# Second sequence's first layer: one product by inner products over pairs of units, and three steps moved to the layer in front

## The chip, the cores and the metric

The kernel runs on one core of one Trainium2 chip. The metric is the device time of that core in microseconds (us), lower is better; the time before is the median of three runs.

## What is computed

Four sequences of 768 rows go through routing attention and then through a feed-forward block. The attention part (8 heads of width 64; a query sees only the keys that fall to the same of 16 centroids) yields `x` with shape (4, 768, 512). The part that the change is about comes after it:

```python
mu = np.mean(x, axis=-1, keepdims=True)
var = np.mean((x - mu) ** 2, axis=-1, keepdims=True)
xn = (x - mu) / np.sqrt(var + 1e-06) * g_ln
ch = np.maximum(xn @ w_ch1, 0.0) @ w_ch2      # 512 -> 2048 -> 512
return (x + ch).astype(np.float32)
```

Everything is float32. The first layer is the product with `w_ch1`, the second the product with `w_ch2`.

## The kernel before

After the attention of all four sequences (b = 0 to 3), the kernel computes the feed-forward block sequence by sequence, first layer, then second layer. Hidden values are kept transposed: 128 hidden channels on the partitions, rows of the sequence in the free dimension.

Both layers use a fast 2 by 2 scheme (seven products of half-size blocks in place of eight). In the first layer of every sequence the halves are: inputs 0 to 255 and 256 to 511, hidden channels 0 to 1023 and 1024 to 2047, rows of the sequence in two halves of 384. A unit j (0 to 7) is 128 hidden channels of each half. Its seven products are the parts 1 to 7 of `first_layer` (L898): each is two float32 matmuls of 128x384 into one PSUM bank (`product`, L851). Part 1 and part 2 together give the hidden tile (0, j): part 1 (`x_ps`) is copied out by ScalarE (ACT) as `p1`, part 2 (`y_ps`) is added to it by VectorE (DVE) in `add_relu` (L885). Part 5 (`z_ps`) and the sums s1 to s4 of blocks of `w1` (`w1_sums`, L647, four DVE instructions of 128x256) and t1 to t4 of blocks of `xn` (`x_sum`) serve the others.

The last two sequences (`paired_layer`, b = 2 and 3) go one level deeper in some of the seven products: two neighbouring units, the two input blocks of 128 and the two halves of the 384 rows form a 2 by 2 scheme again, so that four matmuls of 128x384 become seven of 128x192 (`inner_products`, L1279, its matmul L1287). The operands of that are built by DVE: `inner_x` (L1249, four instructions of 128x192) from the rows, `w_sums` (L1257, four of 128x128) from the weights; each product's result is added onto another or put in its place by DVE (128x192 from PSUM).

The second layer is plain 2 by 2 for b = 0 (`second_layer`, L995) and two levels deep for b = 1 to 3 (`deep_layer`, L1532; 49 products of four matmuls of 128x192). The deep layer reads its weights from DRAM through a ring of ten tiles. What lies there is prepared once: `w2_sum` makes four sums of `w2`, `w2_keep` stores them, `w2_back` reads them again, and `w2_split` (L1065) turns each of seven blocks into four differences (four DVE instructions of 128x512) and stores them to `w2_d` (one DMA of 1 MB on SP).

Order of the work: inside `tc.manual_schedule` the engines named there execute in the order of the source. In the second layer of b = 0 these are TensorE (PE) and DVE; jobs for the gaps stand in the table `jobs` by (part, tt). In the first layer of b = 1 (`first_units`, L1664, and `unit_end`, L1781) they are PE, DVE, ACT and SP. For each unit j the order of parts is 1, 2, then part 4 of unit j - 1, 6, part 3 of unit j - 1, 5, 7. Between them stand: the norm statistics of the next sequence (ACT, L573 to L575), `w1_sums` of the next unit, `outer_sums` of the unit before (L1105), a transpose of columns every second unit (L518), and, at the end of each unit but the last, one `w2_split`, in the order of blocks 1, 5, 3, 4, 2, 7, 6. The check that the shortcut's assumptions hold (`all_in_range`, L806: fourteen short DVE instructions) comes after unit 0, its flag after unit 2.

Room in SBUF: tile `wt` of `w2_split` has two buffers. Pool `splits` is opened where pool `early` of the layer in front is closed, and takes over its room.

Of the kernel before, what the change touches and what calls it, by code (L numbers as in the profile page):

```python
# [23 lines left out]
def kernel(  # L24
# [873 lines left out]
    def first_layer(b, j, part):  # L898
# [26 lines left out]
        elif part == 3:  # L925
            alone = "z" not in st
            if alone:
                st["z"] = ps("y_ps")
            product(st["z"], s4, x_block(b, 1, 1), alone)
            add_relu(1, j, st["z"], st["u2"])  # L930

# [133 lines left out]
    def w2_split(m, src):  # L1065
# [3 lines left out]
        t = splits.tile([P, 4, NQH, P], F32, tag="wt", name="wt", bufs=2)  # L1069
        t1, t2, t3, t4 = [t[:, i] for i in range(4)]  # L1070
        for o, x, y in ((t1, b12, b11), (t2, b22, t1), (t3, b22, b12), (t4, b21, t2)):
            nc.vector.tensor_tensor(o, x, y, ALU.subtract)
        return lambda: nc.sync.dma_start(
            out=w2_d[ORDER.index(m)].rearrange("w p f -> p w f"), in_=t.rearrange("p w c f -> p w (c f)")
        )
# [245 lines left out]

    def deep_room(b):
# [69 lines left out]
    def paired_layer(b):  # L1392
# [67 lines left out]
        def onto_first(j, l):  # L1460
            h = place((1, l))[:, j : j + 2].rearrange("p c t -> p (c t)")
            nc.vector.tensor_tensor(h, fifth_sum, h, ALU.add)
            if l:
                summed.extend(hidden_tile(1, NFH + j + r) for r in range(2))
# [5 lines left out]
        for g in range(NPU):  # L1470
            j = 2 * g
            plan = inner_plan(g, last)
            for slot, (r, part) in enumerate(OUTER[last], 1):
                if (g, slot) != (0, 1):
                    first_layer(b, j + r, part)
                if last and (slot == 7 or slot == 5 and g):
                    onto_first(j, slot // 7)
                for what in plan.get(slot, ()):
# [11 lines left out]
                if not last:  # L1490
                    if g == 0:
# [4 lines left out]
                        if slot == 4:  # L1496
                            x_of[2] = inner_x(x_block(b, 1, 0), pairs_x)
                        if slot == 5:
                            x_sum(b, 4)
                        if slot in (6, 8):  # L1500
                            onto_first(j, slot // 8)
                    elif slot in (5, 7):
                        onto_first(j, slot // 7)
                    if slot == (6 if g else 8):
# [5 lines left out]
                relu(len(summed))  # L1510
# [12 lines left out]
                if g == NPU - 1 and slot in ((6, 8) if last else (9, 10)):  # L1523
                    c = 2 * (slot in (8, 10))
                    inner_sums(deep[b], ORDER[0], cs=slice(c, c + 2))

# [5 lines left out]
    def deep_layer(b, more, st):  # L1532
# [110 lines left out]
        for m, way in STEPS:  # L1643
# [5 lines left out]
            if way == 1:  # L1649
# [12 lines left out]
    deep = {}  # L1662

    def first_units(b, j):  # L1664

        chunks = within.pop(j, []) if b == 0 else []
        for part, ahead in ((1, 0), (2, 0), (4, 1), (6, 0), (3, 1), (5, 0), (7, 0)):
            if chunks and part in (1, 3):
                split_weight(chunks[0])
            if j >= ahead:  # L1670
                first_layer(b, j - ahead, part)
            if part in (4, 6, 3):
                relu(1)
            if b and part == 1 and 0 < j < NT:
                norm_rows(b + 1, j)
            if b and part == 6 and j % 2 and turning:
# [6 lines left out]
            if part == 5:  # L1683
                if j + 1 < NFH:
                    w1_sums(b, j + 1)
                    if b == 0:
                        outer_keep(b, j + 1)
                if b and j:
                    outer_sums(j - 1, j > 4)
# [386 lines left out]
```

## Time and profile before

| what | us |
|---|---|
| median of three runs (876.49 to 877.44) | 876.69 |
| the profiled execution's own time | 876.86 |
| its span in the profile | 874.7 |
| attention, up to the first layer of b = 0 | 0 to 318.7 |
| second layer of b = 0 | 390.0 to 465.1 |
| first layer of b = 1 | 465.1 to 534.9 |
| first layer of b = 2 | 602.5 to 671.4 |

The span is the time from the first to the last recorded instruction. 876.86 less 874.7 is 2.16 us that lie around it. Durations and starts are from this one execution. "Busy" of PE comes from modelled ends of matmuls, so the distance from the start of one group to the start of the next (called pitch below) is the better measure of what a matmul costs. A float32 matmul stands in the trace as two records.

### The profile page before, as it was taken

How to read it: one execution, taken by the hardware profiler on the slowest of the kernel's cores; microseconds unless marked ns; L12 is line 12 of the kernel's file. 1: busy time of each engine (PE TensorE's matmuls, PEld its weight loads, DVE VectorE, ACT ScalarE, POOL GpSimd, SP SyncE). 2: the span in 40 equal slices, each digit the busy share in tenths (PEclk: the TensorE clock that was granted, in tenths of full speed). 3: DMA queues.
4: the chain of work that ended last, by engine and by line, in shares of the span. 5: the costliest groups of instructions: out<-in, count | busy, mean ns of one | idle time of the engine just before them, and what ended most of it. 6: DMA issues, size and time to landing. Idle time of an engine off the chain costs nothing.

```text
span 874.7 us, 13677 instructions
## 1 busy us (share of the span) xinstructions
PE 864.7 (99%) x4768; PEld 590.1 (67%) x4768; DVE 726.0 (83%) x1221; ACT 410.8 (47%) x774; POOL 141.4 (16%) x228
## 2 busy tenths in 40 slices
PE   8999999999999999999999999999999999999996
PEld 5444444444444445568886557998767998778996
DVE  6899999999999878878676878887877897767875
ACT  6777788888888833331003542112563111353110
POOL 1011221222222123220000210002340002350000
PEclk9999999999999999999999999999999999999999
DMA  8777789999986429887685887874567874464865
GB/s 159 140 131 130 135 178 173 206 210 196 208 168 189 122 98 271 257 238 269 163 228 152 269 295 258 283 200 156 156 196 226 295 205 162 134 173 140 274 198 118
DMA packets 229756, 169.65 MB, mean 194 GB/s; under 512 B 159328, under 2 KB 180336, under 8 KB 228656
## 3 DMA queue, kind: packets, MB, share of 16 engines
q1 hardware_dynamic: 194800, 140.50, 58.3%
q0 software_dynamic: 11632, 23.95, 12.4%
q10 hardware_dynamic: 23248, 4.25, 2.7%
q8 instruction: 40, 0.66, 0.3%
q14 instruction: 36, 0.29, 0.1%
HBM read 119.67 MB, written 40.59 MB: 183 GB/s over the span
## 4 chain that ended last, share of the span: by engine, by line
PE 98%; SPq 1%; DMA 1%; issue 0%; ACT 0%; DVE 0%; DVEq 0%
PE x_ps L853 19%; PE s_ps L401 17%; PE a_ps L413 14%; PE x_ps L1161 12%; PE z_ps L1161 6%; PE x_ps L968 5%; PE z_ps L853 5%; PE y_ps L853 4%; PE y_ps L1161 3%; PE x_ps L1287 3%; PE z_ps L968 2%; PE z_ps L1287 1%; PE den_ps L469 1%; PE sim_ps L320 1%; PE y_ps L968 1%; PE y_ps L1287 1%
## 5 line engine op out<-in xcount | busy, mean ns | idle before, releaser
L401 PE MATMUL s_ps<-t,t 64*128 64x384 f32 x768 | 154.8, 483 | 0.0
L401 PEld LDWEIGHTS s_ps<-t,t 64*128 64x128 f32 x768 | 68.0, 187 | 39.0 <-issue 38.3
L1236 POOL DMA_DIRECT2D out_dram<-y x64 | 49.5, 782 | 213.0 <-DVE y L1222 166.7
L1161 PE MATMUL x_ps<-lower,w 128*128 128x192 f32 x448 | 80.5, 326 | 0.0
L1161 PEld LDWEIGHTS x_ps<-lower,w 128*128 128x128 f32 x448 | 74.2, 190 | 0.8
L396 ACT ACTIVATE e<-s_ps 128x768 f32<-128x768 f32 x84 | 67.0, 811 | 7.0 <-PE s_ps L401 6.4
L396 ACT ACTIVATE w<-s_ps 128x768 f32<-128x768 f32 x80 | 64.4, 811 | 8.3 <-PE s_ps L401 7.7
L401 PE MATMUL s_ps<-mask,mask 64*128 64x384 bf16 x384 | 62.8, 323 | 1.0 <-ACT e L396 0.6
L882 ACT COPY p<-x_ps 128x384 f32<-128x384 f32 x32 | 15.3, 477 | 95.3 <-PE x_ps L853 90.0
L413 PE MATMUL a_ps<-e,v_sb 128*64 128x384 f32 x336 | 57.6, 488 | 0.0
L895 ACT ACTIVATE lower<-lower 128x384 f32<-128x384 f32 x88 | 43.7, 518 | 29.1 <-DVE lower L887 19.2
L413 PE MATMUL a_ps<-w,v_sb 128*64 128x384 f32 x320 | 55.2, 488 | 0.0
L853 PE MATMUL x_ps<-xn,w 128*128 128x384 f32 x128 | 46.6, 487 | 0.0
L853 PE MATMUL x_ps<-xn,ws 128*128 128x384 f32 x128 | 46.6, 487 | 0.0
L853 PE MATMUL x_ps<-xt,ws 128*128 128x384 f32 x128 | 46.5, 487 | 0.1
L853 PE MATMUL x_ps<-xt,w 128*128 128x384 f32 x128 | 46.0, 486 | 0.0
L413 PEld LDWEIGHTS a_ps<-e,v_sb 128*64 128x64 f32 x336 | 23.5, 137 | 31.8 <-issue 28.7
L289 POOL DMA_DIRECT2D w<-tb x32 | 28.4, 886 | 90.0 <-DVE tb L286 68.2
L413 PEld LDWEIGHTS a_ps<-w,v_sb 128*64 128x64 f32 x320 | 22.4, 137 | 30.4 <-issue 28.2
L401 PEld LDWEIGHTS <-mask 64*128 64x128 bf16 x384 | 18.9, 94 | 35.0 <-issue 10.0
L1174 ACT COPY u<-x_ps 128x192 f32<-128x192 f32 x30 | 9.6, 318 | 66.4 <-PE x_ps L1161 61.8
L366 ACT ACTIVATE mask<-oh,far 32x384 bf16<-32x384 bf16 x61 | 37.3, 612 | 3.3 <-DVE oh L349 1.9
(314 smaller groups left out, 1840.4 us busy)
## 6 DMA issues: line engine op xcount, KB each, us to landing
w<-w_d SPq DMA_DIRECT2D x84, 256.0 KB, 3.2
raw<-in_moe_w_ch_dram SPq DMA_DIRECT2D x32, 512.0 KB, 5.5
w<-w_t SPq DMA_DIRECT2D x36, 256.0 KB, 5.1
w<-tb POOLq DMA_DIRECT2D x32, 256.0 KB, 5.6
w_d<-wt SPq DMA_DIRECT2D x7, 1024.0 KB, 5.3
w<-w_all SPq DMA_DIRECT2D x27, 256.0 KB, 3.1
v_sb<-in_v_dram SPq DMA_DIRECT2D x32, 192.0 KB, 3.8
xr<-x_d SPq DMA_DIRECT2D x24, 256.0 KB, 3.9
```

Source lines behind the costliest of these rows:

```text
L289: nc.gpsimd.dma_start(out=w, in_=fb, accum_op=ALU.add)
L366: nc.scalar.activation(out, oh[src, :], AF.Identity, bias=add, scale=factor)
L396: nc.scalar.activation(e, s[:, :, :HC], AF.Exp, scale=SCALE)
L401: nc.tensor.matmul(s[:, j, :HC], of_keys[:, keys], of_queries[:, o : o + HC], start=part == first, stop=part != first, skip_group_check=True,)
L413: nc.tensor.matmul(acc[j * D : (j + 1) * D, :HC], loaded[n]["v"][:, j, c, :], e[:, j, :], start=(c == 0), stop=(c == NT - 1),)
L853: nc.tensor.matmul(bank[:, :HC], lhs[:, c, :], rhs[:, c], start=first and c == 0, stop=c == NDH - 1, skip_group_check=True,)
L882: nc.scalar.copy(t, bank[:, :HC])
L895: nc.scalar.activation(h, h, AF.Relu)
L968: nc.tensor.matmul(bank[:, :MH].rearrange("p (h f) -> p h f", h=2), hidden[lhs + (c,)][:, tt * P : (tt + 1) * P], rhs[:, :, c], start=firs ...
L1161: nc.tensor.matmul(bank, w[:, c, :], a[:, c], start=(way in (1, 2, 5) or alone) and c == 0, stop=c == NQH - 1, skip_group_check=True,)
L1236: queues[i % len(queues)].dma_start(out=to, in_=y)
L1287: nc.tensor.matmul(bank, p["w"][way], p["x"][way], start=way in (1, 2, 5), stop=True, skip_group_check=True)
```

## The change

- In the first layer of b = 1, part 2 is no longer made. In its place every pair of units (0 and 1, 2 and 3, and so on) makes the product of the same blocks by seven inner products with `inner_products`, onto the `p1` of both units. `pair_begin` (new) builds their operands: `inner_x` once, `w_sums` once per pair. The order of parts becomes 1, 5, part 4 of unit j - 1, 6, part 3 of unit j - 1, 7, with inner products 1 and 2 after part 6 and 6 and 5 after part 7 of an even unit, 7 after part 5 and 4 and 3 after part 6 of the odd one. `w1_sums` of the next unit comes after part 3 in place of after part 5.
- `w2_split` of blocks 1 and 3 is made in the second layer of b = 0 (`w2_split_ahead`), into two tiles with tag `ws` of two buffers. The others (5, 2, 4, 7, 6) stay, at units 1, 2, 3, 5 and 6; those of units 2 and 6 make two of their four differences one unit later. Each stores 1 MB as two DMAs of 512 KB. Tile `wt` has one buffer in place of two.
- The range check moves to the second layer of b = 0, after product 7 of its second tile.
- `paired_layer`: some steps of b = 2 stand in other slots, and relus are issued one slot later.
- `deep_layer` of b = 1 makes the sums for its first block in its own first steps.

The diff, cut to its core:

```diff
@@ first_layer, part 3, after add_relu(1, j, ...)
+            if alone:
+                summed.pop()
@@
-    def w2_split(m, src):
+    def w2_split(m, src, tiles=None):
...
-        t = splits.tile([P, 4, NQH, P], F32, tag="wt", name="wt", bufs=2)
-        t1, t2, t3, t4 = [t[:, i] for i in range(4)]
-        for o, x, y in ((t1, b12, b11), (t2, b22, t1), (t3, b22, b12), (t4, b21, t2)):
-            nc.vector.tensor_tensor(o, x, y, ALU.subtract)
-        return lambda: nc.sync.dma_start(
-            out=w2_d[ORDER.index(m)].rearrange("w p f -> p w f"), in_=t.rearrange("p w c f -> p w (c f)")
-        )
+        if tiles is None:
+            t = splits.tile([P, 4, NQH, P], F32, tag="wt", name="wt", bufs=1)
+            tiles = [t[:, :2], t[:, 2:]]
+        t1, t2, t3, t4 = [t[:, i] for t in tiles for i in range(2)]
+
+        def make(sums):
+            for o, x, y in sums:
+                nc.vector.tensor_tensor(o, x, y, ALU.subtract)
+
+        make(((t1, b12, b11), (t2, b22, t1)))
+
+        def store():
+            make(((t3, b22, b12), (t4, b21, t2)))
+            for i, t in enumerate(tiles):
+                nc.sync.dma_start(
+                    out=w2_d[ORDER.index(m)][2 * i : 2 * i + 2].rearrange("w p f -> p w f"),
+                    in_=t.rearrange("p w c f -> p w (c f)"),
+                )
+
+        return store
+
+    def w2_split_ahead(m):
+
+        w2_split(m, w2_plain(m), [
+            xpool.tile([P, 4, NDH, P], F32, tag="ws", name="ws", bufs=2).rearrange(
...
+            for _ in range(2)
+        ])()
@@
+    def pair_begin(b, j):
+
+        if j == 0:
+            t = splits.tile([P, 3 * QC], F32, name="pi")
+            pairs_of["parts"] = [t[:, i * QC : (i + 1) * QC] for i in range(3)]
+            pairs_of["x"] = inner_x(x_block(b, 1, 0), splits.tile([P, S], F32, name="xi"))
+            pairs_of["w"] = splits.tile([P, 4 * P], F32, name="wi")
+        (a11, a12), (a21, a22) = blocks = w1_pair(j)
+        w_sums(blocks, parts_of(pairs_of["w"], 4))
+        pairs_of[b, j] = second_pair(
+            b, j, w_operands(a11, a12, a22, pairs_of["w"]), pairs_of["x"], pairs_of["parts"]
+        )
@@ paired_layer, b = 2
+                            inner_keep(3, 0)
...
-                        if slot in (6, 8):
-                            onto_first(j, slot // 8)
+                        if slot in (8, 9):
+                            onto_first(j, slot - 8)
...
-                    if slot == (6 if g else 8):
+                    if slot == 6 and g:
                         inner_keep(3, g)
...
-                relu(len(summed))
+                relu(summed_first)
@@ deep_layer
-            if way == 1:
+            if way == 1 and b < PAIRED and m == ORDER[0]:
+                for cs in (slice(0, NQH - 1), slice(NQH - 1, NQH)):
+                    if cs.start:
+                        inner_sums(st, m, cs=cs)
+                    inner_late(st, m, way, cs)
+            elif way == 1:
@@ first_units
-        for part, ahead in ((1, 0), (2, 0), (4, 1), (6, 0), (3, 1), (5, 0), (7, 0)):
+        parts, sums_after, inner_at = ((1, 0), (2, 0), (4, 1), (6, 0), (3, 1), (5, 0), (7, 0)), 5, {}
+        if b:
+            parts, sums_after = ((1, 0), (5, 0), (4, 1), (6, 0), (3, 1), (7, 0)), 3
+            inner_at = {5: (7,), 6: (4, 3)} if j % 2 else {6: (1, 2), 7: (6, 5)}
+        for part, ahead in parts:
...
+            if part in inner_at:
+                inner_products(pairs_of[b, j - j % 2], inner_at[part])
+                if 3 in inner_at[part]:
+                    summed.extend(hidden_tile(0, j - i) for i in (1, 0))
+                relu(len(summed))
+            if b and part == 1 and j % 2 == 0:
+                pair_begin(b, j)
...
+            if b and part == 6 and halves:
+                halves.pop()()
...
+            if part == (sums_after if j or b == 0 else 6) and j + 1 < NFH:
+                w1_sums(b, j + 1)
...
+            if b and j and part == (3 if j % 2 else 7):
+                outer_sums(j - 1, j > 2)
@@ jobs of the second layer of b = 0
-            (2, 2): [do(norm_rows, 1, 0), do(norm_rows, 1, 1), do(hidden_sums, 4, range(2))],
+            (2, 2): [
+                do(norm_rows, 1, 0), do(norm_rows, 1, 1), do(hidden_sums, 4, range(2)), do(w2_split_ahead, 1),
+            ],
-            (6, 1): [turn_columns],
+            (6, 1): [turn_columns, do(w2_split_ahead, 3)],
-            (7, 1): [do(norm_apply, 1, 0, 2), do(norm_apply, 1, 0, 3)],
+            (7, 1): [do(norm_apply, 1, 0, 2), do(norm_apply, 1, 0, 3), range_check],
@@ unit_end
-                if j == 0:
-                    outer["ends"] = all_in_range()
...
-                m = (1, 5, 3, 4, 2, 7, 6, None)[j]
+                m = (None, 5, 2, 4, None, 7, 6, None)[j]
...
-                if j in (5, 6):
-                    outer_late("s", "e", (0, 0), j - 5)
+                if j == 4:
+                    outer_late("s", "e", (0, 0), 0)
...
-            if b == 1 and m:
-                split()
+            if b == 1:
+                if j % 2 == 0 and m:
+                    halves.append(split)
+                elif m:
+                    split()
```

## Prediction

> **What bounds the kernel now.** I read the page's busy times and the chain, then the stretches around the change, PE's waits, the starts of single matmul groups, and DVE's groups. All lines are of the one profiled execution.
>
> ```profile
> span 874.7 us, 13677 instructions
> PE 864.7 (99%) x4768; PEld 590.1 (67%) x4768; DVE 726.0 (83%) x1221; ACT 410.8 (47%) x774; POOL 141.4 (16%) x228
> ...
> PE 98%; SPq 1%; DMA 1%; issue 0%; ACT 0%; DVE 0%; DVEq 0%
> ```
>
> PE holds the whole chain. Are there gaps in the three stages that the change edits? In the stretches, the columns are length, then busy us of PE, weight load, DVE, ACT:
>
> ```profile
> 390.00:467.50 77.50, 77.50 (x354) 66.73 (x353) 54.13 (x102) 4.33 (x8) 0.00 (x0) 1.00 0.71 203
> 467.50:535.10 67.60, 67.60 (x212) 39.70 (x212) 54.47 (x118) 34.03 (x83) 8.60 (x12) 1.00 0.78 256
> 603.50:671.40 67.90, 67.90 (x269) 47.40 (x268) 53.39 (x133) 38.13 (x103) 18.57 (x24) 1.00 0.58 171
> ```
>
> PE equals the length in each, and the list of PE's waits holds no entry there. Since ends are modelled, I check with starts (start, length, number of records):
>
> ```profile
> 465.05 1.45 PE L853 MATMUL x_ps<-xn,w 128*128 128x384 f32 x4
> 466.34 1.45 PE L853 MATMUL y_ps<-xn,w 128*128 128x384 f32 x4
> 467.63 1.45 PE L853 MATMUL x_ps<-xt,ws 128*128 128x384 f32 x4
> ...
> 619.38 1.45 PE L853 MATMUL x_ps<-xn,w 128*128 128x384 f32 x4
> 620.66 0.49 PE L1287 MATMUL x_ps<-qs 128*128 128x192 f32 x2
> 620.99 0.49 PE L1287 MATMUL z_ps<-qs 128*128 128x192 f32 x2
> 621.32 1.45 PE L853 MATMUL x_ps<-xn,w 128*128 128x384 f32 x4
> ```
>
> A part (two matmuls of 128x384) starts 1.290 after the one before; units of b = 1 follow each other at 9.03 = 7 x 1.290. An inner product takes 0.325 between its neighbours, half of 0.645: a 192-wide matmul pays no extra, also where it stands between wide ones. So this layer is PE work without a gap: time changes by the PE work removed, plus every wait that the change creates.
>
> **What the skill says.** "Perfetto Trace Analysis", Identifying the Most-Contended Engine, warns that matmul busy time is no measure of headroom; hence the starts above. "TensorE: Matmul & The Clock Gate", Step-by-step: what each phase is for, says that the next weights load while a matmul runs; the trace agrees, with 190 ns loads hidden behind 0.162 us records. "VectorE: DVE Perf Modes", TRN2 errata, prices a float32 tensor_tensor at (N + 151)/0.96 ns; the rows below agree (N = 192: 357). "DMA: Bandwidth & Descriptors", Anatomy of one DMA, says that the wait of a DMA is held on the issuing sequencer, so a waiting one holds all behind it on SP; the waits of SP here read that way (L1073 waits 29.7 us in six, for DVE).
>
> **PE, part by part.** Removed: 8 units x 2 matmuls x 0.645 = 10.32. Added: 4 pairs x 7 x 0.325 = 9.10. Net -1.22 us. No other PE work changes; the flag's transpose stays. The operand shapes and the mixture with wide matmuls are those of b = 2, so I see no further price; an unhidden event wait on PE's queue (51 ns, eight in this layer now) is covered there as well.
>
> **DVE in this layer.** Durations:
>
> ```profile
> L1072 DVE TENSOR_TENSOR wt<-w,wt 128x512 f32<-128x512 f32 x6 | 4.1, 688 | 0.1
> L887 DVE TENSOR_TENSOR lower<-y_ps,p 128x384 f32<-128x384 f32 x8 | 4.4, 547 | 2.2 <-PE y_ps L853 2.2
> ...
> L1296 DVE TENSOR_TENSOR pi<-x_ps,p 128x192 f32<-128x192 f32 x12 | 4.3, 356 | 3.9 <-PE x_ps L1287 3.9
> L1265 DVE TENSOR_TENSOR wi<-w 128x128 f32<-128x128 f32 x8 | 2.3, 283 | 0.0
> L1254 DVE TENSOR_TENSOR xi<-xn 128x192 f32<-128x192 f32 x2 | 0.7, 352 | 0.0
> ```
>
> Added: 28 results x 0.356 = 10.0; w_sums 16 x 0.285 = 4.6; inner_x 4 x 0.352 = 1.4; together 16.0. Removed: part 2's adds 8 x 0.547 = 4.4; two splits 8 x 0.687 = 5.5; range check 472.69 to 475.45, 2.8; together 12.7. Net +3.3 on 54.7 of 69.9 (465.05 to 534.94): 58 of 68.7, 84%. Enough room on average, so what counts is order. I laid DVE's order in the new program beside PE's starts at the pitches above:
>
> - Start. `inner_x` writes into room of the closed pool, so it waits until the last `o_sb` store has landed. Before, only the first split (475.67) waited for that. The store is issued at 465.71 and such stores land after 1.8: 467.5. Queued behind on DVE: the sums wi, two results, `w1_sums`(1). Inner 1 and 2 need no sums; s1 of unit 1 is done at 471.0 and wanted at 472.8. Cost 0; the cover is 1.8.
> - PE wants s1 of the next unit after parts 7 and 1, 2.6 after part 3 (5.2 before). The tight place is unit 3: results 4 and 3 (to 496.2), half a split (497.5), transpose (498.4), part 3's add (498.9), s1 at 499.3; PE wants it at 499.5, with its weight load a little earlier. I take 0.1, bounds 0 and 0.4.
> - One `wt` buffer: a split's first instruction now waits for the landing of the store before it. Block 2's stores go out at 497.6; block 4's split is due at 502.3; the 1 MB store's landing in the trace is 5.3:
>
> ```profile
> w_d<-wt SPq DMA_DIRECT2D x7, 1024.0 KB, 5.3
> ```
>
> So 0.6 late, of which 0.4 is cover before PE's inner product 6 of unit 4, which reuses the bank whose result is queued behind. Cost 0.2, bounds 0 and (landing 6.5) 1.4. The distances elsewhere are 6.2 to 6.5 (block 5 to 2, 7 to 6), and over 10 (4 to 7): none late at 5.3.
> - ACT: its copies free the banks; relus that wait for DVE stand behind u2 in odd units and in front of u3. u3 of unit 3 is copied by 500.1, its bank wanted at 500.8. Cost 0.
>
> **What moves to the layer in front.** DVE there is busy 54.1 of 77.5. Two splits (5.5) and the check (2.8) make 62.4. Block 1's split delays the statistics by about 1.5: ready near 425.3, their transpose due at 427.1. In the new SP order the statistics' rows no longer stand behind the store of a `w2` sum (issued 437.03, rows at 437.72, DVE then idle for 4.07 until 443.47); they are issued near 430, so that wait goes and pays for the check. Second tile's product 7 is added before the check; the third's is added by about 447.8, and PE writes its bank again at 451.4. If the rows were as late as before, it would be 450.9: still in time. Block 3's split waits for block 1's stores (made 418.7, wanted 432), and the `ws` room is wanted again only at 463. The two stores pass two row loads and two stores on SP; POOL gets nothing. Cost 0, bounds 0 and 0.5. Deep layer: its first late sum ends near 538.7, wanted at 539.4. Cost 0.
>
> **b = 2.** Its one inner product off the pitch lasts 384 ns against 326: at most 0.06 to gain; the moved DVE steps lie in 53.4 of 67.9. Taken as 0, bounds -0.1 and +0.3.
>
> **Sum.** 876.86 - 1.22 + 0.1 + 0.2 = 875.94 for this execution, span 873.8. The median lies 0.17 below it: 875.8. With the bounds (-1.3 to +0.9 on 876.69): 875.4 to 877.6.
>
> **Rivals.**
> - *DVE becomes the bound through the single `wt` buffer.* If a store lands after 8.2 in place of 5.3, block 4's split is 3.5 late, block 2's 1.7, block 6's 2.0; less covers of 0.4, 1.5 and 1.5, PE waits 3.1 + 0.2 + 0.5 = 3.8: 876.69 - 1.22 + 3.8 = 879.3. It decides against the kernel from a landing of about 7.4 on. For: other transfers in this stretch land after 7.3 to 8.0 (`w_t` of 1 MB, `w` of 256 KB). Against: the store's own 5.3.
> - *More than the PE work is gained.* With no wait at all, b = 2's 0.06 and the run-to-run scatter in its favour (lowest run 0.2 below the median) 875.2; for a gain over 0.2% a hidden stall must go, and starts at exactly 1.290 leave none: 874.8 if there were 0.6 of it.
> - *Nothing is left:* waits of 1.2 at unit 3 and 4 eat the 1.22: 876.7. This lies inside the forecast's class.
>
> **How the numbers follow.** 0.2% of 876.69 is 1.75 us, about what a measurement of this kernel can tell from no change: faster is below 874.94, slower above 878.44. Forecast 0.68, nothing left 0.12 (both within 0.2%, 0.80), DVE bound 0.12 (slower), hidden stall 0.08 (faster). The range 875.0 to 878.2 leaves out the last two, 0.20.
>
> **What would show it.** Right: the layer from the first part of b = 1 to the first deep matmul is 68.9 instead of 69.89, inner products at 0.325, no DVE wait at the statistics' rows near 439, a short DVE wait at block 4's split near 502. Wrong: PE gaps at inner product 6 or part 5 with DVE as releaser; first instructions of splits waiting for DMA by over 2 us; a late transpose of the statistics; a PE gap in the second layer of b = 0; a span that falls by over 1.8.

## The result and the profile after

| | before | after |
|---|---|---|
| median of 21 runs each, side by side | 877.63 us (876.41 to 879.00) | 875.89 us (874.74 to 877.01) |
| ratio of times, 95% interval | | 0.9981 [0.9974, 0.9987] |
| the profiled execution, its span | 876.86, 874.7 | 875.18, 873.4 |

The change gains 1.67 us by the ratio (1.1 to 2.3 by its interval). A gain of 0.92 was forecast, just below this interval. That the forecast of 875.8 us lies close to the measured 875.89 is in part luck, because two differences cancel: the gain was larger than forecast, and the kernel before, 876.69 in the three runs shown, took 877.63 in 21.

The page of the changed kernel reads as that of the kernel before does:

```profile
span 873.4 us, 13780 instructions
...
PE 863.1 (99%) x4792; PEld 593.0 (68%) x4792; DVE 734.7 (84%) x1263; ACT 411.0 (47%) x774; POOL 141.5 (16%) x228
...
PE 95%; DMA 3%; DVE 1%; ACT 0%; issue 0%; ACTq 0%; DVEq 0%
```

Busy PE fell by 1.6 us with 24 more matmul records: fewer long ones, more short ones. The chain (last line) has 3% of DMA where it had 1%: it leaves PE at a new place, which is shown below. The stretches of the three edited stages, cut at the starts of their first matmuls (length, then busy us of PE, weight load, DVE, ACT):

```profile
389.02:464.74 75.72, 75.49 (x347) 65.29 (x346) 60.39 (x123) 3.86 (x7) 0.00 (x0) 1.00 0.78 233
464.74:533.40 68.66, 68.66 (x243) 44.13 (x242) 55.75 (x136) 34.59 (x84) 8.63 (x12) 1.00 0.71 222
600.97:669.76 68.79, 68.79 (x272) 47.77 (x271) 53.65 (x135) 38.20 (x102) 18.62 (x24) 1.00 0.57 173
```

The kernel before, cut in the same way:

```profile
389.84:465.05 75.21, 75.21 (x346) 65.37 (x345) 53.70 (x101) 3.85 (x7) 0.00 (x0) 1.00 0.73 207
465.05:534.94 69.89, 69.89 (x220) 41.06 (x219) 54.73 (x119) 34.51 (x84) 8.60 (x12) 1.00 0.75 249
602.51:671.19 68.68, 68.68 (x271) 47.78 (x271) 53.93 (x135) 38.12 (x102) 18.57 (x24) 1.00 0.58 172
```

So the layer of b = 1 became 1.23 shorter, the second layer of b = 0 took 0.51 more, the layer of b = 2 took 0.11 more. In the first stretch PE is no longer busy from end to end (75.49 of 75.72). PE's groups around the start of the layer of b = 1, then in b = 2 (start, length, records):

```profile
464.74 1.45 PE L853 MATMUL x_ps<-xn,w 128*128 128x384 f32 x4
...
467.32 1.45 PE L853 MATMUL x_ps<-xt,ws 128*128 128x384 f32 x4
468.61 0.49 PE L1314 MATMUL x_ps<-xn,w 128*128 128x192 f32 x2
468.93 0.49 PE L1314 MATMUL y_ps<-xn,w 128*128 128x192 f32 x2
469.26 1.45 PE L853 MATMUL x_ps<-xn,w 128*128 128x384 f32 x4
...
622.63 0.58 PE L1314 MATMUL x_ps<-qs,ws 128*128 128x192 f32 x2
623.05 0.56 PE L1314 MATMUL z_ps<-xt,qs 128*128 128x192 f32 x2
623.44 0.49 PE L1314 MATMUL x_ps<-xn,w 128*128 128x192 f32 x2
```

In b = 1 the pitches are 1.29 and 0.325, as forecast, and no matmul record of the layer starts more than 0.03 off them. In b = 2 two inner products are followed after 0.42 and 0.39 in place of 0.325: 0.16 more, which is that stage's loss (before had one such, 0.06).

DVE's groups that were priced, in the layer of b = 1 (busy, mean ns, idle before with its releasers), and the store of the splits (KB, us to landing):

```profile
L887 DVE TENSOR_TENSOR lower<-z_ps,u 128x384 f32<-128x384 f32 x14 | 7.7, 551 | 1.8 <-ACT u L882 1.0 <-PE z_ps L853 0.6
...
L1078 DVE TENSOR_TENSOR wt<-w_t,wt 128x512 f32<-128x512 f32 x8 | 5.5, 688 | 0.1
L1078 DVE TENSOR_TENSOR wt<-w_t 128x512 f32<-128x512 f32 x8 | 5.4, 678 | 0.0
L1323 DVE TENSOR_TENSOR pi<-x_ps,p 128x192 f32<-128x192 f32 x12 | 4.2, 350 | 0.9 <-PE x_ps L1314 0.9
...
L1281 DVE TENSOR_TENSOR xi<-xn 128x192 f32<-128x192 f32 x2 | 0.7, 354 | 1.8 <-DMA out_dram<-o_sb 1.8
```

```profile
w_d<-wt SPq DMA_DIRECT2D x10, 512.0 KB, 3.4
```

The wait of `inner_x` for the last output store is there at its forecast size (1.8). No split waits for a store of `wt`: the idle time before them is 0.0 and 0.1.

Where do the 0.51 us of the first stretch come from? PE's groups at part 4 of that layer:

```profile
443.52 7.07 PE L970 MATMUL x_ps<-w2t,lower 128*128 128x256 f32 x32
450.82 1.35 PE L970 MATMUL x_ps<-w2t,lower 128*128 128x256 f32 x5 [0.23 <-DVE o_sb L982]
```

The bracket is an idle time of PE and its releaser: DVE's addition L982, which empties the bank. It shows only part of the loss. By their starts the record at 450.82 comes 0.61 after the one ahead of it and the next one 0.32 later, where all the others follow at 0.216: together that is the 0.5. A PE gap in this stage was one of the signs of being wrong that the prediction named. What kept DVE:

```profile
437.27 0.42 DVE L994 TENSOR_TENSOR o_sb<-z_ps,o_sb 128x256 f32<-128x256 f32 x1
442.53 0.98 DVE L518 STREAM_TRANSPOSE turned<-col 128x768 f32<-128x768 f32 x1 [4.83 <-DMA col<-xT_d]
443.43 1.78 DVE L616 TENSOR_TENSOR xn<-xn,stat_row 128x768 f32<-128x768 f32 x2
...
447.66 0.35 DVE L810 TENSOR_REDUCE ends<-rdens 128x1 f32<-128x192 f32 x1
...
450.26 0.16 DVE L821 TENSOR_TENSOR ends<-ends 128x1 f32<-128x1 f32 x1
450.34 0.42 DVE L982 TENSOR_TENSOR o_sb<-x_ps,xb 128x256 f32<-128x256 f32 x1
```

The range check (447.66 to 450.4) stands ahead of the addition. The wait for the statistics' rows is gone, as forecast, but DVE now idles 4.83 us for the columns (`col`) instead, and the check came after it. The chain in order of time (start, length, what) leads on to why the columns were late:

```profile
426.45 0.26 ACT st L605
...
426.73 1.28 DMA stat_d<-st
...
428.02 4.81 DMA stat_row<-stat_d
...
432.85 9.59 DMA col<-xT_d
```

The columns' load leaves ACT's queue in the moment in which the first load of the statistics' rows lands (432.83), and then takes 9.59 us. In the kernel before it left at 427.92, ahead of the rows (437.72), and the copy of the statistics `st` stood behind it:

```profile
427.92 0.57 ACTq L534 DMA_DIRECT2D col<-xT_d  x1
428.53 0.25 ACT L605 COPY st<-stat_ps 12x128 f32<-12x128 f32 x1 [5.31 <-DMA x_d<-turned]
```

In the changed kernel the copy comes first (426.45), so the rows are loaded earlier, and that holds back what DVE needs next.

My theory for the experiments: PE's work bounds the layer of b = 1, the splits had to leave it, the check costs by its place in the layer in front, and what remains of the 1.67 (some 1 us by this one profile) is scatter of stages that the change doesn't touch. Rivals: the gain there is real; DVE's load as a whole decides.

### The profile page after: what moved, and what is told of

Same layout as the page of the kernel before. It is cut to its first block, busy times and chain, and to the rows that moved or that the text cites. A ratio compares the mean times of both kernels' runs of the same rounds, so it can differ in the third digit from the quotient of the medians.

```text
span 873.4 us, 13780 instructions
## 1 busy us (share of the span) xinstructions
PE 863.1 (99%) x4792; PEld 593.0 (68%) x4792; DVE 734.7 (84%) x1263; ACT 411.0 (47%) x774; POOL 141.5 (16%) x228
## 4 chain that ended last, share of the span: by engine, by line
PE 95%; DMA 3%; DVE 1%; ACT 0%; issue 0%; ACTq 0%; DVEq 0%
PE x_ps L853 19%; PE s_ps L401 18%; PE a_ps L413 14%; PE x_ps L1188 12%; PE z_ps L1188 6%; PE z_ps L853 5%; PE x_ps L1314 4%; PE y_ps L1188 3%; PE z_ps L970 2%; PE y_ps L853 2%; PE x_ps L970 2%; PE z_ps L1314 2%; PE sim_ps L320 1%; PE den_ps L469 1%; PE y_ps L970 1%; DMA col<-xT_d 1%
## 5 line engine op out<-in xcount | busy, mean ns | idle before, releaser
L1201 ACT COPY u<-x_ps 128x192 f32<-128x192 f32 x30 | 9.6, 319 | 65.9 <-PE x_ps L1188 61.3
```

## The experiments

All fourteen profiles in one table. Stage lengths are differences of the starts of the first matmuls of the stages; "around" is the profiled execution's time less its span (spans are on record to 0.1, so it is good to 0.05). The later stages, from the deep layer of b = 1 to PE's last group (at 867.26 in the kernel before), are equal within 0.02 us in all of them, except for the column of b = 2; from that group to the end of the span it is 7.1 to 8.2.

| kernel | start of second layer, b = 0 | second layer, b = 0 | first layer, b = 1 | first layer, b = 2 | around | median (runs) |
|---|---|---|---|---|---|---|
| before | 389.84 | 75.21 | 69.89 | 68.68 | 2.16 | 877.63 (21) |
| before_again | 391.42 | 75.21 | 69.88 | 68.68 | 2.12 | 877.64 (13) |
| two_stores | 390.72 | 75.21 | 69.88 | 68.62 | 2.31 | 877.71 (1) |
| moved_only | 390.61 | 75.29 | 69.88 | 68.63 | 1.91 | 877.82 (13) |
| pair_only | 390.13 | 75.21 | 70.42 | 68.88 | 1.88 | 877.79 (13) |
| splits_inside | 390.99 | 75.21 | 70.38 | 68.83 | 1.82 | 878.22 (1) |
| check_inside | 390.09 | 75.21 | 68.67 | 68.78 | 1.80 | 875.40 (1) |
| after | 389.02 | 75.72 | 68.66 | 68.79 | 1.78 | 875.89 (21) |
| after_again | 392.04 | 75.38 | 68.66 | 68.78 | 1.82 | 876.17 (21) |
| one_store | 390.03 | 75.22 | 68.66 | 68.81 | 1.78 | 875.98 (1) |
| twice | 390.53 | 75.21 | 72.56 | 68.78 | 1.74 | 880.04 (1) |
| check_early | 390.84 | 75.22 | 68.66 | 68.79 | 1.84 | 876.05 (13) |
| early_b2 | 389.93 | 75.21 | 68.67 | 68.71 | 1.76 | 875.11 (9) |
| early_b2_again | 390.82 | 75.21 | 68.67 | 68.63 | 1.85 | 875.62 (9) |

### The kernel before, once more

No edit.

> The kernel before once more, unchanged. The median fell by 1.67 us, of which the starts of the matmul groups give 1.23 in the edited layer, and give back 0.5 in the second layer of the first sequence and some 0.2 later; about 1 us stands in stages that the change doesn't touch (0.37 ahead of the first layer, 0.45 in the first layer of the first sequence, where the profile before had two longer gaps). If that is scatter of one profiled execution, this profile shows these two stages anywhere between the two seen (318.3 to 318.7 and 70.7 to 71.2), and the ratio of times is 1.000 within 0.0007. If the changed kernel gains there for a reason, this profile repeats 318.65 and 71.19 within 0.05.

Measured: 0.9996 [0.9988, 1.0004]; the second layer of b = 0 starts at 391.42, 1.6 later than in the first profile. Over all profiles that start lies between 389.02 and 392.04, the two ends of this range being two executions of the same changed kernel. This is more scatter than was expected. So the 0.8 us that the changed kernel's first profile gained ahead of the edited stages, against the first profile of the kernel before, is scatter, as are the 2.2 that its second one lost there. The three edited stages of the kernel before repeat within 0.01.

### The moves alone

```diff
-            (2, 2): [do(norm_rows, 1, 0), do(norm_rows, 1, 1), do(hidden_sums, 4, range(2))],
+            (2, 2): [
+                do(norm_rows, 1, 0), do(norm_rows, 1, 1), do(hidden_sums, 4, range(2)), do(w2_split_ahead, 1),
+            ],
...
-            (6, 1): [turn_columns],
+            (6, 1): [turn_columns, do(w2_split_ahead, 3)],
...
-            (7, 1): [do(norm_apply, 1, 0, 2), do(norm_apply, 1, 0, 3)],
+            (7, 1): [do(norm_apply, 1, 0, 2), do(norm_apply, 1, 0, 3), range_check],
...
-                if j == 0:
-                    outer["ends"] = all_in_range()
...
-                m = (1, 5, 3, 4, 2, 7, 6, None)[j]
+                m = (None, 5, 2, 4, None, 7, 6, None)[j]
```

Each split is stored by two DMAs here as well; `wt` keeps its two buffers.

> Of the change only the moves: two splits of w2 and the range check stand in the second layer of the first sequence; the product of part 2 stays a plain one, and splits keep two buffers. My account: the layer of the second sequence keeps its 69.89 us (PE work without a gap), the second layer of the first sequence has 75.7 in place of 75.2, since the third tile's part 4 waits for the check on DVE; time about 0.5 above before (+0.2 to +0.8). Rival: the 0.5 in that stage belongs to something else in the change or to scatter, and the moves cost nothing: 75.2 and 0.0.

Measured: 0.9998 [0.9989, 1.0006], the second layer 75.29, the layer of b = 1 69.88. My size was too large: 0.08, not 0.5. DVE's order is the same as in the changed kernel, but the columns landed 0.4 earlier in the stage:

```profile
443.69 0.98 DVE L518 STREAM_TRANSPOSE turned<-col 128x768 f32<-128x768 f32 x1 [4.41 <-DMA col<-xT_d]
```

443.69 is 53.08 after this stage's start (390.61); in the changed kernel it was 53.51. The layer of b = 1 gains nothing when work leaves DVE: it was not bound there.

### The inner products alone

```diff
             (2, 2): [
-                do(norm_rows, 1, 0), do(norm_rows, 1, 1), do(hidden_sums, 4, range(2)), do(w2_split_ahead, 1),
+                do(norm_rows, 1, 0), do(norm_rows, 1, 1), do(hidden_sums, 4, range(2)),
             ],
...
-            (6, 1): [turn_columns, do(w2_split_ahead, 3)],
+            (6, 1): [turn_columns],
...
-            (7, 1): [do(norm_apply, 1, 0, 2), do(norm_apply, 1, 0, 3), range_check],
+            (7, 1): [do(norm_apply, 1, 0, 2), do(norm_apply, 1, 0, 3)],
...
+                if j == 0:
+                    range_check()
...
-                m = (None, 5, 2, 4, None, 7, 6, None)[j]
+                m = (1, 5, 3, 4, 2, 7, 6, None)[j]
```

The changed kernel makes `outer_sums` for `s` from unit 3 on, in room of `w2`; block 2, split after unit 4, is therefore split from other numbers here, by the same instructions. The output is then not the right one; the run is of use for its times alone.

> The change without the moves: the inner products stand in the layer of the second sequence, and both splits and the range check stay in that layer too. DVE then has 58.0 + 5.5 + 2.8 = 66.3 us of work in 68.7 (97%). Theory that the moves are needed: DVE falls behind, PE waits for s1 and for banks, and the layer takes 70 to 73 us: time 1 to 4 above the changed kernel, so from no change to 2.5 above before. Rival, that only PE's work counts as long as DVE's sum fits: the layer takes 68.7, the second layer of the first sequence is back at 75.2, and the time is 0.5 below the changed kernel.

Measured: 0.9996 [0.9988, 1.0005], 1.7 above `check_early`, which ran beside it (876.05). The layer takes 70.42: 1.76 lost, 1.24 at a first place and 0.51 at a second of the same kind (inner product 4 of units 1 and 5). The first:

```profile
476.00 1.45 PE L853 MATMUL x_ps<-xt,ws 128*128 128x384 f32 x4
478.36 0.59 PE L1314 MATMUL x_ps<-xi,w 128*128 128x192 f32 x2 [0.91 <-DVE pi L1323]
478.79 0.56 PE L1314 MATMUL z_ps<-xn,wi 128*128 128x192 f32 x2
479.18 1.45 PE L853 MATMUL z_ps<-xn,ws 128*128 128x384 f32 x4
```

The inner product starts 2.36 after the part ahead of it in place of 1.29, and it and the next are stretched (0.43 and 0.39). PE waits for the bank whose result L1323 takes, which stands on DVE behind the range check and half a split:

```profile
473.95 0.34 DVE L810 TENSOR_REDUCE ends<-rdens 128x1 f32<-128x192 f32 x1
...
476.63 0.68 DVE L1078 TENSOR_TENSOR wt<-w 128x512 f32<-128x512 f32 x1
...
477.96 0.35 DVE L1323 TENSOR_TENSOR pi<-x_ps,p 128x192 f32<-128x192 f32 x1
```

The rival that only sums matter falls: DVE is busy 62.5 of 70.4 us in this layer, 89%, and still late at two points.

### The check alone, and the splits alone, put back

`check_inside`:

```diff
-            (7, 1): [do(norm_apply, 1, 0, 2), do(norm_apply, 1, 0, 3), range_check],
+            (7, 1): [do(norm_apply, 1, 0, 2), do(norm_apply, 1, 0, 3)],
...
+                if j == 0:
+                    range_check()
```

> The changed kernel with the range check back in the layer of the second sequence (behind its first unit), the two splits still ahead. The kernel without both moves lost 1.76 in this layer, in front of the inner products of the first pair (0.91 of waiting for DVE's result, then two stretched matmuls) and of the third pair. By DVE's order the check (2.7) ends 0.1 behind the point where PE is ready for the pair's result: the layer takes 68.7 to 68.9 and the second layer of the first sequence 75.2. If the check alone is what DVE has no room for, the layer takes 69.5 to 70.4.

`splits_inside` (block 3, split after unit 4 as a whole, is made from other numbers, for the same reason and with the same result as above):

```diff
             (2, 2): [
-                do(norm_rows, 1, 0), do(norm_rows, 1, 1), do(hidden_sums, 4, range(2)), do(w2_split_ahead, 1),
+                do(norm_rows, 1, 0), do(norm_rows, 1, 1), do(hidden_sums, 4, range(2)),
             ],
...
-            (6, 1): [turn_columns, do(w2_split_ahead, 3)],
+            (6, 1): [turn_columns],
...
-            (7, 0): [turn_columns, do(norm_apply, 1, 0, 0), do(norm_apply, 1, 0, 1)],
-            (7, 1): [do(norm_apply, 1, 0, 2), do(norm_apply, 1, 0, 3), range_check],
+            (7, 0): [range_check, turn_columns, do(norm_apply, 1, 0, 0), do(norm_apply, 1, 0, 1)],
+            (7, 1): [do(norm_apply, 1, 0, 2), do(norm_apply, 1, 0, 3)],
...
-                m = (None, 5, 2, 4, None, 7, 6, None)[j]
+                m = (1, 5, 2, 4, 3, 7, 6, None)[j]
...
                 if j == 4:
+                    split()
...
-                if j % 2 == 0 and m:
+                if j in (0, 2, 6):
                     halves.append(split)
-                elif m:
+                elif m and j != 4:
                     split()
```

> The changed kernel with both splits back in the layer of the second sequence (blocks in the order 1, 5, 2, 4, 3, 7, 6) and the range check ahead of the columns' transpose in the layer in front. DVE has 58 + 5.5 = 63.5 us in 68.7 here. If room on average is what decides, the layer takes 68.7; if order decides, one half split before the first pair's result stays inside the 2.15 us that DVE waited there, and the whole split of block 3 behind unit 4 makes the third pair late by up to 0.7: 68.7 to 69.5.

Measured: with the check inside the layer takes 68.67 and the second layer of b = 0 75.21: the check had room where it was. With the splits inside the layer takes 70.38: 1.72 lost, all at one inner product of unit 5, more than the 0.7 that I had allowed:

```profile
512.48 1.46 PE L853 MATMUL x_ps<-xt,ws 128*128 128x384 f32 x4
515.32 0.59 PE L1314 MATMUL x_ps<-xi,w 128*128 128x192 f32 x2 [1.38 <-DVE pi L1323]
```

What DVE did in this time, and the busy times of the layer:

```profile
511.51 0.68 DVE L1078 TENSOR_TENSOR wt<-w 128x512 f32<-128x512 f32 x1
...
514.91 0.35 DVE L1323 TENSOR_TENSOR pi<-x_ps,p 128x192 f32<-128x192 f32 x1
```

```profile
466.20:536.58 70.38, 69.00 (x243) 44.06 (x242) 60.37 (x143) 34.34 (x84) 8.61 (x12) 1.00 0.74 245
```

The four differences of block 3 (511.5 to 514.1) and a sum stand on DVE ahead of the result that frees the bank. DVE is busy 60.4 of 70.4, 86%; with the check inside it is busy 57.9 of 68.7, 84%, and not late at all. Order decides, not the share. The two moves also act together. At the first pair the check alone costs nothing (`check_inside`) and half a split alone costs nothing (`splits_inside`), but both cost 1.24 (`pair_only`). At the third pair a whole split costs 1.72, half a split 0.51. So in both kernels that leave the splits inside the products don't pay, and once the splits are moved, the check's move is worth 0.01. Both splits inside by halves, with the check moved, was not run; as an estimate from these figures that kernel loses 0.51, and moving the splits would then be worth 0.5 in place of 1.7.

### The check one step earlier

```diff
-            (7, 0): [turn_columns, do(norm_apply, 1, 0, 0), do(norm_apply, 1, 0, 1)],
-            (7, 1): [do(norm_apply, 1, 0, 2), do(norm_apply, 1, 0, 3), range_check],
+            (7, 0): [range_check, turn_columns, do(norm_apply, 1, 0, 0), do(norm_apply, 1, 0, 1)],
+            (7, 1): [do(norm_apply, 1, 0, 2), do(norm_apply, 1, 0, 3)],
```

> The changed kernel with the range check one step earlier on DVE: ahead of the transpose of the columns at which DVE idled for 4.83 us (437.7 to 442.5), so that it stands in that idle time. If the check's place makes the third tile's part 4 late: the wait of PE for o_sb there goes, the stage takes 75.2 in place of 75.72, and the time is 0.5 below the changed kernel (0.3 to 0.7). If the stage is long for another reason (the loads, the two splits), nothing changes: 0.0.

Measured: 0.9979 [0.9970, 0.9987]; the second layer of b = 0 takes 75.22. DVE makes the check inside the idle time:

```profile
442.03 0.16 DVE L821 TENSOR_TENSOR ends<-ends 128x1 f32<-128x1 f32 x1
443.71 0.98 DVE L518 STREAM_TRANSPOSE turned<-col 128x768 f32<-128x768 f32 x1 [1.51 <-DMA col<-xT_d]
```

The columns land late here as well; the idle time before L518 falls from 4.83 to 1.51 with the check in it. The 2.7 us of the check no longer follow L518, so PE's bank is emptied that much sooner. This run alone doesn't show that the check's place was the cause: L518 starts 52.87 after the stage's start here, which is earlier than in the changed kernel's first profile (53.51). The next section settles it. The time beside the changed kernel's (0.9981) can't tell 0.5 apart.

### The changed kernel once more

No edit.

> The changed kernel once more, unchanged. By the traces the stages that the change edits give -1.23 (first layer of the second sequence), +0.11 (first layer of the third) and +0.5 at the third tile's part 4, if the columns' load lands as late as in the first profile. If that landing varies (the kernel with the moves alone had it 0.4 earlier after the stage's start and lost only 0.08), this profile has the second layer of the first sequence between 75.2 and 75.8, and the ratio to before is 0.9985 to 0.9990. If the whole 1.67 is the change's work, the ratio is again 0.9981 and the two early stages are short again (318.3 and 70.7).

Measured: 0.9983 [0.9976, 0.9989]: a gain of 1.5 us, with the early stages long this time (392.04). It is a little more than the stages alone were expected to give (0.9985 to 0.9990). Its second layer takes 75.38. With the check in its changed place there are five profiles: 75.72, 75.38, 75.29 (moves alone), 75.22 (`one_store`) and 75.21 (`twice`). The cost is 0 to 0.5, 0.15 on average; the first profile showed the worst of them. It follows the arrival of the columns: L518, which waits for them, starts 53.51, 53.16, 53.08, 52.10 and 52.70 after the stage's start, so from about 53.0 on each tenth that they come later is a tenth lost. The kernels with the check elsewhere (`check_early`, `check_inside`, both of `early_b2`) have 75.21 or 75.22, `early_b2_again` with a start of L518 after 53.30, between two that lost 0.17 and 0.51. So the check's place is the cause, and the columns' arrival sets the size. In all nine profiles with the splits ahead their load leaves within 0.1 us of the landing of the first load of rows, 43.5 to 44.1 us after the stage's start; in the others it leaves after 37.8 to 38.1. The landing differs too. The issues in 20 us of that stage, the changed kernel and then `two_stores`, which has the splits inside (KB each, median us to landing):

```profile
w_d<-ws SPq DMA_DIRECT2D x2, 512.0 KB
...
col<-xT_d ACTq DMA_DIRECT2D x1, 384.0 KB, 9.6
```

```profile
col<-xT_d ACTq DMA_DIRECT2D x2, 384.0 KB, 3.8
```

The first such load lands after 7.3 to 9.6 with the splits ahead (3.8 to 4.1 in the three profiles without them that have its landing). With the splits ahead, the two stores of block 3 (issued at 432.54) run beside it. That they are what makes it long was not tried apart. Why the two loads wait for each other, though they share no tile, stands in the records: in all nine, the columns' load waits for semaphore 104, which is also the one that it counts up when it lands, and the transfer before it that counts up 104 is this first load of rows. In the five other profiles it has semaphore 107, last used by a store of the turned columns on ACT's own queue. So, by the records, a transfer on SP's queue held one on ACT's queue through a shared semaphore; a kernel with another number was not run.

### One store or two for each split

`one_store`, the changed kernel (`whole` is the tile `wt`; the two splits made ahead keep their two stores):

```diff
+            if whole is not None:
+                nc.sync.dma_start(
+                    out=w2_d[ORDER.index(m)].rearrange("w p f -> p w f"),
+                    in_=whole.rearrange("p w c f -> p w (c f)"),
+                )
+                return
             for i, t in enumerate(tiles):
```

> The changed kernel with one store of 1 MB for each split of w2, as before, in place of two of 512 KB. In the changed kernel the first half of block 2 left at 492.8 and the second near 497.0, and block 4's split (501.66, 112.6 after the layer before last began) waited for nothing. If the halves are what kept the single buffer from costing: the one store leaves near 497.0 after the same start, lands 5.3 later (near 502.3), the first difference of block 4 waits 0.4 to 0.8 for it, and PE loses 0 to 0.3: layer 68.66 to 68.96. If DVE's better order alone did it, no difference waits and the layer is 68.66. The time around the span: 2.15 as before if the two stores per split are what shortened it to 1.77, else 1.77.

`two_stores`, the kernel before:

```diff
-        return lambda: nc.sync.dma_start(
-            out=w2_d[ORDER.index(m)].rearrange("w p f -> p w f"), in_=t.rearrange("p w c f -> p w (c f)")
-        )
+        def store():
+            for i in (0, 2):
+                nc.sync.dma_start(
+                    out=w2_d[ORDER.index(m)][i : i + 2].rearrange("w p f -> p w f"),
+                    in_=t[:, i : i + 2].rearrange("p w c f -> p w (c f)"),
+                )
+
+        return store
```

> The kernel before with each split's store as two DMAs of 512 KB, nothing else changed. The time around the span was 2.15 in all 84 runs of the kernel before (2.10 to 2.60 in them) and near 1.77 in every kernel with new code, the one with the moves alone and the one with the products alone among them; these two have the halved stores in common. If the stores are the cause: 1.7 to 1.9 here. If it is something else that they share: 2.15. The stages keep their lengths (75.2, 69.88, 68.68) in both cases.

Measured: with one store the first difference of block 4 waits, but briefly, and PE loses nothing (68.66):

```profile
502.43 0.69 DVE L1079 TENSOR_TENSOR wt<-w_t 128x512 f32<-128x512 f32 x1 [0.17 <-DMA w_d<-wt]
```

So the halves do remove a wait, of 0.17 us, and the work beside it would have covered that. The time around the span is 1.78 in `one_store` and 2.31 in `two_stores`: the number of stores is not what shortened it.

### Three inner products of each pair made twice

```diff
+            for _ in range(2 if p.get("twice") and way in (1, 2, 5) else 1):
                 nc.tensor.matmul(
                     bank, p["w"][way], p["x"][way], start=way in (1, 2, 5), stop=True, skip_group_check=True
                 )
...
+        pairs_of[b, j]["twice"] = True
```

> The changed kernel with three of the seven inner products of each pair in the second sequence's first layer made twice (they overwrite the same bank, so the output stays): 12 more matmuls of 128x192. If PE's work bounds the layer and a narrow matmul costs 0.325 between wide ones: 68.66 + 12 x 0.325 = 72.56 (72.5 to 72.65). If waits for DVE or ACT filled part of the layer unseen, part of the addition is hidden: below 72.3.

Measured: 72.56, that is 3.90 for 12 matmuls, 0.325 each. The doubled ones are followed after 0.65:

```profile
469.61 0.81 PE L1315 MATMUL x_ps<-xn,w 128*128 128x192 f32 x4
470.26 0.81 PE L1315 MATMUL y_ps<-xn,w 128*128 128x192 f32 x4
470.91 1.45 PE L853 MATMUL x_ps<-xn,w 128*128 128x384 f32 x4
```

Added PE work goes through in full: no wait hides in the layer.

### Early check, and the third sequence as before

```diff
@@ jobs of the second layer of b = 0
-            (7, 0): [turn_columns, do(norm_apply, 1, 0, 0), do(norm_apply, 1, 0, 1)],
-            (7, 1): [do(norm_apply, 1, 0, 2), do(norm_apply, 1, 0, 3), range_check],
+            (7, 0): [range_check, turn_columns, do(norm_apply, 1, 0, 0), do(norm_apply, 1, 0, 1)],
+            (7, 1): [do(norm_apply, 1, 0, 2), do(norm_apply, 1, 0, 3)],
@@ paired_layer, b = 2
-                        if slot in (8, 9):
-                            onto_first(j, slot - 8)
+                        if slot in (6, 8):
+                            onto_first(j, slot // 8)
...
-                relu(summed_first)
+                relu(len(summed))
```

> The changed kernel with the range check ahead of the columns' transpose, and with the order of steps in the first layer of the third sequence as in the kernel before. Account by stage: 75.2 in the second layer of the first sequence, 68.66 in the first layer of the second, 68.65 in that of the third (68.79 with the edits); sum -1.25 against before, ratio 0.9986. If the edits in the third sequence are needed by what goes before them, that stage is longer than 68.8.

> The kernel with the early range check and the third sequence's order as before, once more: 0.9972 [0.9962, 0.9982] came from 9 runs. Account by the stages (75.2, 68.66, 68.7: -1.2) and by the time around the span (-0.38): -1.6, ratio 0.9982, that is 0.2 to 0.5 below the changed kernel. If the low value was a real further gain: 0.9972 again and a stage that is shorter by 0.8.

Measured: 0.9972 [0.9962, 0.9982], then 0.9978 [0.9968, 0.9988]. The layer of b = 2 takes 68.71 and 68.63; every profile with the edits there has 68.78 to 68.88, those without 68.62 to 68.71. The edits of b = 2 cost 0.12 (68.79 against the mean of 68.67 here). By the stages this kernel is shorter than the changed one by 0.12 + 0.15 on average, and its medians (875.11 and 875.62 against 875.89 and 876.17) lie in that direction; the intervals overlap, so it isn't shown to be faster by the time. No stage is shorter by 0.8: the low first value was not a further gain.

## Why the prediction was right, point by point

- **PE, -1.22.** Right: 1.23 (69.89 to 68.66), seven of seven times in kernels where nothing else stood in the way or was added, and `twice` gave the price of 0.325 again. (The 0.162 us that the prediction calls a record is the distance between the starts of two records; a record lasts 0.326.)
- **DVE in the layer, net +3.3.** Too large, without effect: busy time rose by 1.0 (54.73 to 55.75). The sum took the length of each record, but back-to-back records overlap: those of 128x192 last 0.35 and can start 0.27 apart. Added up, the lengths rose by 2.3 (61.1 to 63.4), and the overlap grew by 1.3. The last 1.0 of the 3.3 was not traced. That order decides and not the share was right, and both experiments with splits inside show it.
- **Start of the layer, cost 0.** Right: `inner_x` waited 1.82 and PE didn't.
- **Unit 3, 0.1.** It was 0: s1 of the next unit was done at 498.62 and PE used it at 499.07, 0.45 later, where 0.2 was laid out.
- **The single `wt` buffer, 0.2.** It was 0. I let both stores of block 2 leave with the last difference at 497.6. The first left at 492.77, when its own two differences were made, and the second near 497. `one_store` shows the step as I had thought it: the wait is 0.17 in place of 0.6, inside the cover of 0.4.
- **The moves in front, cost 0, bounds 0 and 0.5.** The step that failed in its reasoning is "so that wait goes and pays for the check". The rows came in time, and what was late next was the columns' load. I had followed the moved stores past what stands on SP and POOL, but not what the earlier statistics do on ACT's queue. DVE still idled 4.83 us ahead of the check (4.49 and 4.41 in two other profiles), so product 7 of the third tile was added 61.3 us after the stage's start (450.34), where 58.0 was laid out. Cost: 0 to 0.51, 0.15 on average of five.
- **b = 2, 0.** It costs 0.12, inside the bounds.
- **The sum.** -1.23 + 0.15 + 0.12 = -0.96 in the span, where -0.92 was forecast: three small terms were off and nearly cancel. What the prediction didn't see at all is the time around the span, a term that it took as equal without a word: 2.15 in the median of 41 runs of the kernel before and 1.79 in 21 of the changed one, ranges 2.11 to 2.39 and 1.72 to 1.86. That is -0.36. Together -1.32, inside the interval of the gain (1.1 to 2.3) and of its repetition (1.0 to 2.1). The 0.2 to 0.35 left are less than these intervals can tell.
- **The rivals.** The bound through `wt` needed landings over 7.4; the halves took 2.8 to 6.7 and the whole stores 4.8 to 5.2. A hidden stall wasn't there (`moved_only`, `twice`). "Nothing is left" is what `pair_only` and `splits_inside` came to, by PE waiting for a bank: with the splits inside as these two place them, the products cost 0.5 more than they save.

**Open:** what shortens the time around the span. The moves alone (1.82 in the median of 13) and the products alone (1.78) both have the short one; the halved stores by themselves do not. In the code no further edit was found that the two share and that acts before the first or after the last recorded instruction. The traces give one lead, which does not settle it: in the two profiles of the kernel before, in `two_stores` and in `moved_only`, one 8 KB transfer of the queue that the page calls "instruction" starts 1.3 to 1.7 after the last recorded instruction, and in the ten others none does; but `moved_only` has it and is short. Open are also why the matmuls after a wait are stretched, and what makes the columns' load take 7.3 to 9.6.

## What to carry to other kernels

When a kernel is bound by one engine without gaps, price work on that engine by starts of groups, and for every other engine look for the one place where its result frees what the bound engine wants next: 86% busy DVE was late there and 84% was not, and moving 5.5 us of its work one layer ahead was worth 1.7 against the arrangement tried with that work inside. Put moved work into the idle time ahead of a wait, not behind it, since a wait that goes away may only uncover the next. Two pieces of work that each fit alone can be late together, so put them back one by one and both at once. Before explaining a gain below 0.2%, take a second profile of both kernels and compare stage by stage: unedited early stages here differed by 3 us between two executions of one kernel, while its edited layer of b = 1 repeated within 0.01.

## What the runs showed that I had not expected

- The time around the span differs between kernels. The medians of the sets of runs are 2.15 to 2.18 us for the kernel before and 1.75 to 1.82 for those with the moves or the products; single runs reach 2.75 on both sides (`before_again`, `moved_only`).
- After PE has waited for a bank, the narrow matmul that starts then and the one behind it take 0.43 and 0.39 in place of 0.325 (`pair_only`, `splits_inside`): 0.17 on top of the wait. The same pattern, without an idle time shown, makes up the loss in b = 2.
- Two transfers on different queues can wait for each other though they share no tile, by the semaphore that both count up (nine of nine profiles with the splits ahead, none of the five others).
- Records of DVE last longer than they keep the engine: 128x192 from SBUF lasts 0.35, as the price in the Trainium skill's "VectorE: DVE Perf Modes", TRN2 errata, gives it, but the next one starts after 0.27; 128x512 lasts 0.69 and the next starts after 0.61. Where the next reads what the one before wrote, it starts only after 0.39 and 0.72 in this trace. A sum of durations is therefore not the time for which the engine is held.
